# All softmax sums of an attention unit in one TensorE block: column groups by head and half, the fifth key block's values earlier

## The chip, the core and the metric

The kernel runs on one NeuronCore of a Trainium2 chip, in one launch. Times are device microseconds (us) of an execution. The engines are TensorE (PE in the profile; PEld is its weight load), VectorE (DVE), ScalarE (ACT), GpSimd (POOL) and SyncE (SP, which here only issues DMAs). Each works through its own queue in the order of the program; semaphores tie them together.

## What is computed

Sliding-window attention with a linear bias by distance, then a mixture-of-experts layer in which each token goes to one of 8 experts, all in float32:

```python
# q, k, v: (8, 8, 576, 64)
scores = scale * np.matmul(q, k.transpose(0, 1, 3, 2))
bias = slopes[:, None, None] * (-np.abs(rel).astype(np.float32))[None, :, :]
mask = (rel >= 0) & (rel < window)                       # window 128
scores = np.where(mask, scores + bias[None], -1000000000.0)
attn = np.exp(scores - np.max(scores, axis=-1, keepdims=True))
attn = attn / (np.sum(attn, axis=-1, keepdims=True) + 1e-09)
x = np.matmul(attn, v)                                   # -> (4608, 512)
...
h = np.maximum(x_sorted[lo:hi] @ w1[e], 0.0)             # the rows of expert e
y_sorted[lo:hi] = h @ w2[e]
...
return gate_w[:, None] * y
```

## The kernel before

**Units.** Attention is cut into 16 units. A unit `u` is two batch entries (`bp` is the pair, 0 to 3) and two heads (`hp` is the pair, 0 to 3), so four units in a row make one pair of batch entries. The 576 positions are nine key blocks of 64 (`kb`). A key block meets three query blocks of 64: its own and the next two. The queries are cut in two halves, `QH`: half 0 has 320 columns, half 1 has 256. Key blocks 0 to 4 reach into half 0, blocks 3 to 8 into half 1.

**Steps of a unit.**
- `scores` (matmuls at L790): q times k for one group of two key blocks (three in the last), as 64x64 matmuls, four of them side by side on the four quarters of the array. ACT takes the exponential (L799, L809), DVE multiplies by the bias factors (L803); the result is a probability tile `pe` of six buffers. Nothing is divided yet.
- `values` (L833): probabilities times v, again 64x64, into `at`, a PSUM tile with one buffer.
- `finish`: ACT copies `at` to SBUF (L850, L852). Then the sums of the probabilities over the keys (L864): matmuls of the probability tile with `ind`, 128 rows by 32 columns of weights, so that each writes 32 of the 128 output partitions, here called a column group (0 to 3). Head `r` and the parity of the key block choose the group: `j = 2 * r + kb % 2`. Half 0 begins with two matmuls of zeros (`none`), since odd key blocks don't reach its first 64 columns. ACT or DVE adds the result to `sumT` (L873, L875). The PSUM tile of the sums, `m`, has two buffers and is shared with the tasks below.

**Order.** The order is written out by hand (`manual_schedule`): each engine runs its instructions as the loop over `i = 4u + g` issues them. At step `g` of unit `u`:
- g = 0: one group of scores, values of key blocks 0, 1 (half 0)
- g = 1: values 2, 3 (half 0); a task; scores
- g = 2: values 4 (half 0); `finish(u, 0)`; a task; scores; values 3, 4, 5 (half 1)
- g = 3: values 6, 7, 8 (half 1); `finish(u, 1)`; a task; scores

Scores are issued ahead of their use: four groups, in units 0 and 1 three (L1417). SP's loads of the unit after the next are paced by probability tiles.

**Tasks.** When the four units of a pair of batch entries are done, `behind(bp)` (L1353) makes a list that `some()` (L1383) works off, one entry at each step: the gate's logits (`gate`, L884 matmuls in the same 128x32 shape as the sums, to groups 0 to 3 in turn; DVE adds L889, L891), their transposes on TensorE (`turn`, L908), routing on DVE, and the rows of x, transposed and written to DRAM. For `bp = 0` the rows are transposed on DVE (`squares_turned`, L1123) into tiles of the pool `rows`, which has four buffers; POOL copies the scales in (L1131) and issues the DMAs (L1142). The last of these nine tiles, tile 8, is left to the list of `bp = 1`, as `last` (L1374), which begins at unit 8. `scale_a` (L911) adds the two partial sums of a head, which lie in different column groups.

After the attention come the experts (two levels of seven-product matrix multiplication), with TensorE matmuls at L1527, L1590, L1629 and L1646. The change does not touch them.

Of the kernel before, what the change touches and what calls it, by code (L numbers as in the profile page):

```python
# [8 lines left out]
F32 = mybir.dt.float32  # L9
# [4 lines left out]
ALU = mybir.AluOpType  # L14
PSUM = bass.MemoryType.PSUM

P = 128
# [441 lines left out]
def kernel(  # L459
# [12 lines left out]
    nc = tc.nc  # L472
# [9 lines left out]
    KB = P // 2  # L482
    NK = S // KB
# [23 lines left out]
    with ExitStack() as fast:  # L507
# [70 lines left out]
        QH = [(0, 5 * KB), (5 * KB, 4 * KB)]  # L578

        ac = pool(att, "att_consts", 1)  # L580
# [9 lines left out]
        units = [(bp, hp) for bp in range(BP) for hp in range(HP)]  # L590
# [64 lines left out]
        for b in range(2):  # L655
            half = slice(b * KB, (b + 1) * KB)
# [14 lines left out]
        fac = ac.tile([P, H, GC], F32, name="fac")  # L671
# [17 lines left out]
        ind = ac.tile([P, HP, 32], F32, name="ind")  # L689
        nc.gpsimd.memset(ind[:], 0.0)  # L690
        for hp in range(HP):
            for b in range(2):
                nc.gpsimd.memset(ind[b * KB : (b + 1) * KB, hp, 16 + 2 * hp + b : 17 + 2 * hp + b], 1.0)
        none = ac.tile([P, 32], F32, name="none")
        nc.gpsimd.memset(none[:], 0.0)
        ident = consts.tile([P, P], F32, name="ident")
        make_identity(nc, ident[:])

# [80 lines left out]
        prob, xT, sumT, gs = {}, {}, {}, {}  # L779
# [34 lines left out]
        def by_distance(x, kb, a, b):  # L814

            if kb == NK - 1:
                return x[:, 5 * KB :].rearrange("p (j x) -> p j x", j=1)
            return x.rearrange("p (j k x) -> p j k x", j=3, k=2)[:, a:b, kb % 2, :]
# [22 lines left out]
        def finish(u, half):  # L841

            bp, hp = units[u]
            q0, qn = QH[half]
            if hp == 0 and half == 0:
                xT[bp] = xp.tile([P, HP, 2 * S], F32, name="xT")
                sumT[bp] = xp.tile([P, S], F32, name="sumT")
            acc = at.pop((u, half))[0]
            n = min(q0 + qn, LQ) - q0
            nc.scalar.copy(xT[bp][:, hp, : 2 * LQ].rearrange("p (b q) -> p b q", b=2)[:, :, q0 : q0 + n], acc[:, :, :n])  # L850
            if n < qn:
                nc.scalar.copy(xT[bp][:, hp, 2 * LQ :].rearrange("p (b q) -> p b q", b=2), acc[:, :, n:qn])  # L852
            sm = ps_m.tile([P, 512], F32, name="m")
            ops = []
            for kb in range(max(0, q0 // KB - 2), (q0 + qn) // KB):
                lo, hi = max(q0, kb * KB), min(q0 + qn, (kb + 3) * KB)
                ops.append((kb % 2, lo, hi, prob[4 * u + min(kb // 2, 3)], (kb, lo // KB - kb, hi // KB - kb)))
            if half == 0:
                ops.insert(0, (1, 0, KB, None, None))
            begun = set()  # L860
            for par, lo, hi, pe, at_kb in ops:
                for r in range(2):
                    j = 2 * r + par
                    nc.tensor.matmul(  # L864
                        sm[32 * j : 32 * j + 32, lo - q0 : hi - q0].rearrange("p (j x) -> p j x", x=KB),
                        lhsT=none[:] if pe is None else ind[:, hp, :],
                        rhs=fac[:, 0:1, :KB] if pe is None else by_distance(pe[:, r, :], *at_kb),
                        start=j not in begun, stop=True, skip_group_check=True,
                    )
                    begun.add(j)  # L870
            to = sumT[bp][:, q0 : q0 + qn]
            if hp == 0:
                nc.scalar.copy(to, sm[:, :qn])  # L873
            else:
                nc.vector.tensor_tensor(to, sm[:, :qn], to, op=ALU.add)  # L875


        def gate(bp, c):
            if bp not in gs:
# [31 lines left out]
        def scale_a(bp):  # L911
            G = gsr[bp]

            s = small.tile([P, TPB, 2, HP], F32, name="s")
            Gs = G.rearrange("p t (a k x) -> p t a k x", a=2, k=2)
            for t0, t1, p0, p1, b in ((0, 4, 0, P, 0), (4, 8, 0, P, 1), (8, 9, 0, KB, 0), (8, 9, KB, P, 1)):
                nc.vector.tensor_tensor(
                    s[p0:p1, t0:t1, :, :], Gs[p0:p1, t0:t1, :, 0, 16 + b : 24 + b : 2],
                    Gs[p0:p1, t0:t1, :, 1, 16 + b : 24 + b : 2], op=ALU.add,
                )  # L920
            low = small.tile([P, TPB * H], F32, name="low")
            sf = s.rearrange("p t a h -> p (t a h)")
            nc.vector.tensor_scalar(low[:], sf, scalar1=SUM_LO, scalar2=None, op0=ALU.is_ge)
            nc.vector.scalar_tensor_tensor(
                low[:], in0=sf, scalar=SUM_HI, in1=low[:], op0=ALU.is_le, op1=ALU.mult,
            )
            nc.vector.tensor_reduce(bad[:, bp : bp + 1], low[:], axis=AX, op=ALU.min)
            s_of[bp] = s
# [424 lines left out]
        def behind(bp):  # L1353

            g3 = [lambda k=k: gate(bp, k) for k in range(3)]
            t3 = [lambda k=k: turn(bp, k) for k in range(3)]
            rs = [lambda t=t: row(bp, t) for t in range(TPB)]
            a, a2, b, b2, c, n, q, p, p2, o, o2, e = (
                [lambda f=f: f(bp)] for f in (
                    scale_a, scale_a2, scale_b, scale_b2, scale_c, count, scales_squared, place, place2, ones_at,  # L1360
                    ones_at2, enlist,
                )
            )
            if bp == 0:
                rt = [lambda t=t: squares_turned(bp, t) for t in range(TPB)]
                ro = [
                    lambda t=t: (squares_scaled(bp, t), squares_out(bp, t, nc.gpsimd)) for t in range(TPB)
                ]
                return [g3[0:1], g3[1:2], g3[2:] + t3[0:1], t3[1:], a, a2, b, b2, c + n, rt[0:1], q + p + rt[1:2],
                        p2 + rt[2:4] + ro[0:2], o + ro[2:4], o2, rt[4:6] + ro[4:5], e + rt[6:8] + ro[5:8]]  # L1370
            rt, ro = ([lambda t=t, f=f: f(bp, t) for t in range(TPB)] for f in (row_turned, row_out))
            if bp == 1:
                last = [lambda: squares_turned(0, TPB - 1), lambda: squares_scaled(0, TPB - 1),
                        lambda: squares_out(0, TPB - 1, nc.gpsimd)]  # L1374
                return [g3[0:1], g3[1:2], g3[2:] + t3[0:1] + last, t3[1:], a + rt[0:1], a2 + rt[1:2], b + rt[2:3],
                        b2 + rt[3:4], c + n, [], p + ro[0:2], p2 + ro[2:4] + rs[4:5], o + rs[5:6], o2 + rs[6:7], rs[7:8],
                        e + rs[8:9]]
            return [g3, t3, a + a2, b + b2 + rt[0:1], c + n + rt[1:2], rt[2:4], p + p2 + ro[0:4], o + o2 + rs[4:6],
                    rs[6:9] + [early_holes], e + [early_table, lambda: gather(fixed[0], x_d[: 3 * 2 * S, :])]]
# [22 lines left out]
        for i in range(NG):  # L1402
            u, g = divmod(i, 4)
            bp, hp = units[u]
            if u + 2 < len(units):
                no_earlier_than(prob[i + 1][0:1, 0, 0:1])
                load_part(u + 2, g)
            if u in (10, 11) and g % 2 == 1:
                d = 2 * (u - 10) + g // 2
                load_w1(fixed[0], w1_a, slice(d, d + 1))  # L1410
            if i == 1:
                token_numbers()
                table_consts()
            if i == 12:
                token_parts()

            ahead = i + (3 if u < 2 else 4)  # L1417
            if g == 0:
                scores_to(ahead)
            if g == 0:  # L1420
                values(u, 0, (0, 1))
                if u < HP - 1:
                    factors(u + 1)
            elif g == 1:
                values(u, 0, (2, 3))
            elif g == 2:
                values(u, 0, (4,))
                finish(u, 0)
                some()
                scores_to(ahead)  # L1430
                values(u, 1, (3, 4, 5))
            else:
                values(u, 1, (6, 7, 8))
                finish(u, 1)
            if u in (13, 14):
                ws_tasks.pop(0)()
            if u == len(units) - 1 and g == 1:
                first = [t for _, t in prepare(fixed[0])]
                tasks.extend(first[:3])
            if g != 2:  # L1440
                some()
            if g in (1, 3):
                scores_to(ahead)
            if g == 3 and hp == HP - 1 and bp < BP - 1:
                tasks.extend(behind(bp))
# [270 lines left out]
        for i in range(len(groups)):  # L1716
# [3 lines left out]
            if i == 0:  # L1720
                strassen1(g, start=with_tail)
                todo = [t for _, t in prepare(fixed[1])]
                sums = [f for (f,) in todo[9:]]
# [64 lines left out]
```

## Time and profile before

| | us |
|---|---|
| median of 3 runs | 681.19 (678.4 to 684.45) |
| profiled execution | 676.36 |
| its span, first to last instruction | 674.6 |
| granted TensorE clock in it | 0.995 of full |

An instruction row of the profile's timeline reads: start, length, engine, line, operation, output and inputs, rows by columns of the weights for matmuls, shape, how many were merged, and in brackets the idle time of the engine before it with what ended that. A row of the groups reads: how many, busy time, mean duration in ns, idle time before them. A row of the waits reads: total, times, longest. Each float32 matmul shows as two rows of weight load and matmul. Ends of matmuls are modelled, and they overlap, so durations add up to more than the time that passes.

### The profile page before, as it was taken

The numbers are of one execution on the slowest core, as the hardware profiler recorded it, in microseconds if no ns is written. First come the engines' busy times: TensorE is split into PE (matmuls) and PEld (weight loads), VectorE is DVE, ScalarE is ACT, GpSimd is POOL, SyncE is SP. The second block draws the span as 40 slices with busy tenths as digits, with TensorE's granted clock in tenths as the row PEclk, the third lists the DMA queues.
The fourth block names the chain that finished last, engine by engine and source line by source line (L and its number), as shares of the span: only waits on it lengthen the run. The fifth ranks groups of instructions, "written<-read, shape, count | busy, mean of one in ns | idle before, by whom it ended". The sixth has DMA issues, their size and how long they took to land.

```text
span 674.6 us, 14825 instructions
## 1 busy us (share of the span) xinstructions
PE 648.4 (96%) x6004; PEld 541.2 (80%) x6004; DVE 362.1 (54%) x727; ACT 215.8 (32%) x493; POOL 272.7 (40%) x458
## 2 busy tenths in 40 slices
PE   6899999999999999999999999999999999999994
PEld 5768868687888888878878897889788788878892
DVE  3345956697797758436623841474356337614410
ACT  5757666675330331123012211311231023113100
POOL 8000682234032683575156426624760665230020
PEclk9999999999999999999999999999999999999998
DMA  9875998974358924673195439235822864282010
GB/s 267 226 190 170 256 246 256 374 217 133 125 121 304 332 62 145 215 284 110 63 313 178 149 93 320 98 141 191 302 63 99 281 218 148 60 298 112 1 64 8
DMA packets 55104, 122.02 MB, mean 181 GB/s; under 512 B 5905, under 2 KB 21425, under 8 KB 55026
## 3 DMA queue, kind: packets, MB, share of 16 engines
q1 hardware_dynamic: 43074, 92.51, 42.8%
q0 software_dynamic: 10800, 27.58, 12.8%
q8 instruction: 49, 0.80, 0.5%
q10 hardware_dynamic: 1152, 0.88, 0.4%
q14 instruction: 29, 0.24, 0.1%
HBM read 101.79 MB, written 19.96 MB: 180 GB/s over the span
## 4 chain that ended last, share of the span: by engine, by line
PE 74%; issue 10%; DVE 6%; DMA 3%; POOL 2%; ACT 1%; DVEq 0%; POOLq 0%; SPq 0%; ACTq 0%
PE pair1a L1590 5%; PE pair1b L1590 5%; PE pair0b L1527 4%; PE pair0a L1527 4%; PE pair2a L1527 4%; PE pair0a L1590 4%; PE pair0b L1590 4%; PE pair1b L1527 4%; PE pair2b L1527 4%; PE pair1a L1527 4%; PE pair2b L1590 4%; PE pair2a L1590 4%; PE sp L790 4%; PE at L833 3%; PE pair0a L1646 2%
## 5 line engine op out<-in xcount | busy, mean ns | idle before, releaser
L1278 POOL DMA_INDIRECT xg<-x_rows,p_idx x124 | 132.5, 1068 | 35.7 <-issue 33.3
L1613 POOL DMA_INDIRECT out_dram<-zo,s_idx x39 | 44.6, 1144 | 174.3 <-DVE zo L1604 136.8
L803 DVE TENSOR_TENSOR pe<-pe,fac 128x512 f32<-128x512 f32 x64 | 43.5, 686 | 46.0 <-ACT pe L799 45.1
L790 PE MATMUL sp<-q_sb,k_sb 64*64 64x192 f32 (+2 forms) x1152 | 54.9, 320 | 8.5 <-DMA q_sb<-in_qT_dram 5.7
L833 PE MATMUL at<-pe,v_sb 64*64 64x192 f32 (+2 forms) x1408 | 53.8, 282 | 2.4 <-issue 1.6
L833 PEld LDWEIGHTS at<-pe,v_sb 64*64 64x64 f32 x1408 | 45.6, 134 | 10.4 <-issue 3.6
L790 PEld LDWEIGHTS sp<-q_sb,k_sb 64*64 64x64 f32 x1152 | 39.9, 136 | 17.1 <-issue 5.8
L799 ACT ACTIVATE pe<-sp 128x512 f32<-128x512 f32 x64 | 38.5, 601 | 28.4 <-issue 12.1
L809 ACT ACTIVATE pe<-sp,mid 128x128 f32<-128x128 f32 x128 | 40.2, 374 | 0.0
L1538 ACT ACTIVATE h<-h 128x512 f32<-128x512 f32 x32 | 20.2, 630 | 38.6 <-DVE h L1537 38.6
L864 PE MATMUL m<-pe,ind 128*32 128x192 f32 (+2 forms) x704 | 29.4, 286 | 0.6 <-issue 0.6
L1142 POOL DMA_DIRECT2D x_rows<-xs x48 | 26.0, 553 | 7.3 <-DVE w L540 2.3
L1473 POOL COPY paced_by<-h 1x1 f32<-1x1 f32 x48 | 18.4, 383 | 23.0 <-DVE h L1637 16.5
L1296 DVE TENSOR_TENSOR xn<-xg 128x512 f32<-128x512 f32 x39 | 26.2, 674 | 2.5 <-DMA xg<-x_rows,p_idx 1.6
L864 PEld LDWEIGHTS m<-pe,ind 128*32 128x32 f32 x704 | 23.1, 109 | 2.9 <-issue 0.9
L1131 POOL COPY xs<-sq 128x16 f32<-128x16 f32 x10 | 3.2, 321 | 53.9 <-ACT sq L1109 53.9
L1312 DVE STREAM_TRANSPOSE xgT<-xn 128x512 f32<-128x512 f32 x31 | 22.1, 711 | 1.1
L538 DVE TENSOR_TENSOR w2s<-w 128x512 f32<-128x512 f32 x16 | 11.0, 685 | 20.5 <-DMA w<-in_moe_w_dram 20.5
L850 ACT COPY xT<-at 128x640 f32<-128x640 f32 (+1 forms) x32 | 19.0, 593 | 9.0 <-PE at L833 6.5
L1646 PE MATMUL pair2a<-w,h 128*128 128x512 f32 x48 | 21.1, 592 | 0.0
L1527 PE MATMUL pair0a<-xgT,w 128*128 128x256 f32 x72 | 17.1, 380 | 0.0
L1527 PE MATMUL pair0b<-xgT,w 128*128 128x256 f32 x72 | 17.1, 380 | 0.0
(381 smaller groups left out, 1407.7 us busy)
## 6 DMA issues: line engine op xcount, KB each, us to landing
w<-in_moe_w_dram SPq DMA_DIRECT2D x29, 2048.0 KB, 8.8
k_sb<-in_kT_dram SPq DMA_DIRECT2D x15, 576.0 KB, 7.8
q_sb<-in_qT_dram SPq DMA_DIRECT2D x15, 576.0 KB, 5.3
v_sb<-in_v_dram SPq DMA_DIRECT2D x14, 320.0 KB, 4.7
x_rows<-xs POOLq DMA_DIRECT2D x16, 264.0 KB, 5.2
v_sb<-in_v_dram SPq DMA_DIRECT2D x14, 256.0 KB, 4.6
x_rows<-xs POOLq DMA_DIRECT2D x32, 66.0 KB, 4.8
x_rows<-xT SPq DMA_DIRECT2D x8, 264.0 KB, 5.8
```

What stands on the lines that cost most here:

```text
L790: nc.tensor.matmul(by_distance(sp[c * KB : (c + 1) * KB, r, :GC], kb, 0, n), lhsT=k_sb[u][hs, c, kb * KB : (kb + 1) * KB], rhs=q_sb[u][hs, ...
L799: nc.scalar.activation(outer, sp[:, :, :GC].rearrange("p r (j x) -> p r j x", j=3)[:, :, 0:3:2, :], AF.Exp, scale=SCALE,)
L803: nc.vector.tensor_tensor(outer, outer, fac[:, h0 : h0 + 2, : 2 * w].rearrange("p r (j x) -> p r j x", j=2)[:, :, :, : 2 * KB], op=ALU.mult,)
L809: nc.scalar.activation(pe[:, r, inner], sp[:, r, inner], AF.Exp, bias=mid[:, h0 + r : h0 + r + 1], scale=SCALE,)
L833: nc.tensor.matmul(acc[r * D : (r + 1) * D, c, lo - q0 : hi - q0].rearrange("p (j x) -> p j x", x=KB), lhsT=v_sb[u // 2][c * KB : (c + 1) ...
L864: nc.tensor.matmul(sm[32 * j : 32 * j + 32, lo - q0 : hi - q0].rearrange("p (j x) -> p j x", x=KB), lhsT=none[:] if pe is None else ind[:, ...
L1278: nc.gpsimd.indirect_dma_start(out=to, out_offset=None, in_=where, in_offset=bass.IndirectOffsetOnAxis(ap=idx, axis=0),)
L1296: nc.vector.tensor_tensor(xn[:], x, s.unsqueeze(3).to_broadcast([P, NA, HP, TQ]), op=ALU.mult)
L1527: nc.tensor.matmul(ps[:, f * 256 : (f + 1) * 256], lhsT=left[m][:, d, fb * P : (fb + 1) * P], rhs=right[m][:, d, :], start=(m in (1, 2, 5) ...
L1590: nc.tensor.matmul(ps[:, :256], lhsT=left[m][:, f, c * P : (c + 1) * P], rhs=right[m][:, f, :], start=(m in (1, 2, 5) and f == 0), stop=Tr ...
L1613: ins = nc.gpsimd.indirect_dma_start(out=out[:, :], out_offset=bass.IndirectOffsetOnAxis(ap=s_idx[:, g["c0"] + j : g["c0"] + j + 1], axis= ...
L1646: nc.tensor.matmul(ps[:], lhsT=g["h"][:, fb, :], rhs=g["w2"][:, fb, :], start=(fb == 0), stop=(fb == FB - 1),)
```

## The change

The sums leave `finish` and become a function of their own, `sums(u)`, issued once a unit, at the beginning of g = 2: all key blocks, and in each the halves that it reaches. The column group is now chosen by half and head, `j = 2 * half + r`. Each group then receives all the key blocks of its head and half, the matmuls of zeros go away, and one PSUM tile holds the sums of the whole unit: half 0 in partitions 0 to 63, half 1 in 64 to 127. `sumT` keeps the same layout, and POOL sets the parts to zero that no sum reaches. Two evacuations of 64 partitions take the place of two of 128. `scale_a` adds the pairs of columns that now belong together.

The values of key block 4 move from g = 2 to g = 1, and `finish(u, 0)`, now only the copies, follows them there, ahead of that step's task and scores. In the list of `bp = 1`, `last` moves from the third entry to the first.

```diff
@@ finish / sums
             if hp == 0 and half == 0:
                 xT[bp] = xp.tile([P, HP, 2 * S], F32, name="xT")
                 sumT[bp] = xp.tile([P, S], F32, name="sumT")
+                for k in range(2):
+                    q0, qn = QH[1 - k]
+                    nc.gpsimd.memset(sumT[bp][k * KB : (k + 1) * KB, q0 : q0 + qn], 0.0)
...
+        def sums(u):
+
+            bp, hp = units[u]
             sm = ps_m.tile([P, 512], F32, name="m")
-            ops = []
-            for kb in range(max(0, q0 // KB - 2), (q0 + qn) // KB):
-                lo, hi = max(q0, kb * KB), min(q0 + qn, (kb + 3) * KB)
-                ops.append((kb % 2, lo, hi, prob[4 * u + min(kb // 2, 3)], (kb, lo // KB - kb, hi // KB - kb)))
-            if half == 0:
-                ops.insert(0, (1, 0, KB, None, None))
             begun = set()
-            for par, lo, hi, pe, at_kb in ops:
-                for r in range(2):
-                    j = 2 * r + par
-                    nc.tensor.matmul(
-                        sm[32 * j : 32 * j + 32, lo - q0 : hi - q0].rearrange("p (j x) -> p j x", x=KB),
-                        lhsT=none[:] if pe is None else ind[:, hp, :],
-                        rhs=fac[:, 0:1, :KB] if pe is None else by_distance(pe[:, r, :], *at_kb),
-                        start=j not in begun, stop=True, skip_group_check=True,
-                    )
-                    begun.add(j)
-            to = sumT[bp][:, q0 : q0 + qn]
-            if hp == 0:
-                nc.scalar.copy(to, sm[:, :qn])
-            else:
-                nc.vector.tensor_tensor(to, sm[:, :qn], to, op=ALU.add)
+            for kb in range(NK):
+                for half in range(2):
+                    q0, qn = QH[half]
+                    lo, hi = max(q0, kb * KB), min(q0 + qn, (kb + 3) * KB)
+                    if lo >= hi:
+                        continue
+                    pe = prob[4 * u + min(kb // 2, 3)]
+                    for r in range(2):
+                        j = 2 * half + r
+                        nc.tensor.matmul(
+                            sm[32 * j : 32 * j + 32, lo - q0 : hi - q0].rearrange("p (j x) -> p j x", x=KB),
+                            lhsT=ind[:, hp, :], rhs=by_distance(pe[:, r, :], kb, lo // KB - kb, hi // KB - kb),
+                            start=j not in begun, stop=True, skip_group_check=True,
+                        )
+                        begun.add(j)
+            for half in range(2):
+                q0, qn = QH[half]
+                rows_of = slice(half * KB, (half + 1) * KB)
+                to = sumT[bp][rows_of, q0 : q0 + qn]
+                if hp == 0:
+                    nc.scalar.copy(to, sm[rows_of, :qn])
+                else:
+                    nc.vector.tensor_tensor(to, sm[rows_of, :qn], to, op=ALU.add)
@@ scale_a
-                    s[p0:p1, t0:t1, :, :], Gs[p0:p1, t0:t1, :, 0, 16 + b : 24 + b : 2],
-                    Gs[p0:p1, t0:t1, :, 1, 16 + b : 24 + b : 2], op=ALU.add,
+                    s[p0:p1, t0:t1, :, :], Gs[p0:p1, t0:t1, 0, :, 16 + b : 24 + b : 2],
+                    Gs[p0:p1, t0:t1, 1, :, 16 + b : 24 + b : 2], op=ALU.add,
@@ behind
-                return [g3[0:1], g3[1:2], g3[2:] + t3[0:1] + last, t3[1:], a + rt[0:1], a2 + rt[1:2], b + rt[2:3],
+                return [last + g3[0:1], g3[1:2], g3[2:] + t3[0:1], t3[1:], a + rt[0:1], a2 + rt[1:2], b + rt[2:3],
@@ the loop
             elif g == 1:
-                values(u, 0, (2, 3))
+                values(u, 0, (2, 3, 4))
+                finish(u, 0)
             elif g == 2:
-                values(u, 0, (4,))
-                finish(u, 0)
+                sums(u)
                 some()
                 scores_to(ahead)
                 values(u, 1, (3, 4, 5))
```

More of the change, by code (lines that the diff above doesn't have):

```diff
@@ L693 @@
                 nc.gpsimd.memset(ind[b * KB : (b + 1) * KB, hp, 16 + 2 * hp + b : 17 + 2 * hp + b], 1.0)
-        none = ac.tile([P, 32], F32, name="none")
-        nc.gpsimd.memset(none[:], 0.0)
         ident = consts.tile([P, P], F32, name="ident")
```

## The prediction

> **What bounds the kernel now.** I read the page's engine shares and its chain of waits first, then the busy time by stretch, then TensorE's groups with shapes kept apart, then the timeline of single units.
>
> ```profile
> PE 648.4 (96%) x6004; PEld 541.2 (80%) x6004; DVE 362.1 (54%) x727; ACT 215.8 (32%) x493; POOL 272.7 (40%) x458
> PE 74%; issue 10%; DVE 6%; DMA 3%; POOL 2%; ACT 1%; DVEq 0%; POOLq 0%; SPq 0%; ACTq 0%
> 11.00:36.00 25.00, 18.99 (x512) 15.98 (x501) 8.84 (x14) 17.50 (x47) 5.64 (x54) 1.00 0.88 230
> 36.00:167.00 131.00, 125.67 (x2947) 101.77 (x2950) 89.24 (x225) 87.47 (x230) 44.94 (x91) 1.00 0.78 234
> 167.00:674.60 507.60, 497.69 (x2468) 418.58 (x2458) 259.76 (x470) 104.97 (x205) 212.96 (x270) 0.99 0.49 163
> ```
>
> The columns of the last three rows are the stretch, its length, and the busy time of PE, PEld, DVE, ACT and POOL. TensorE sets the end. The change lies in the attention, which ends near 167 us. From 36 us on PE is busy 125.67 of 131 us, so PE time added there reaches the end and PE time saved there mostly does. Before 36 us PE waits a quarter of the time while the DMA share is 0.88: units 0 to 2 are held by their loads, so I count 13 of the 16 units (3 to 15).
>
> ```profile
> L864 PE MATMUL m<-pe,ind 128*32 128x192 f32 x320 | 23.4, 328 | 0.0
> L864 PE MATMUL m<-pe,ind 128*32 128x128 f32 x192 | 19.3, 277 | 0.6 <-issue 0.6
> L864 PE MATMUL m<-pe,ind 128*32 128x64 f32 x192 | 13.9, 223 | 0.0
> 155.58 0.29 PE L833 MATMUL at<-pe,v_sb 64*64 64x64 f32 x8
> 155.81 0.25 PE L864 MATMUL m<-fac,none 128*32 128x64 f32 x2
> 155.82 0.36 PE L864 MATMUL m<-pe,ind 128*32 128x192 f32 x2
> 155.88 0.23 PE L864 MATMUL m<-fac,none 128*32 128x64 f32 x2
> 155.94 0.83 PE L864 MATMUL m<-pe,ind 128*32 128x192 f32 x18
> 156.70 0.88 PE L790 MATMUL sp<-q_sb,k_sb 64*64 64x192 f32 x16
> 157.58 1.55 PE L833 MATMUL at<-pe,v_sb 64*64 64x64 f32 x48
> 159.06 0.86 PE L864 MATMUL m<-pe,ind 128*32 128x64 f32 x24
> 159.85 1.54 PE L790 MATMUL sp<-q_sb,k_sb 64*64 64x192 f32 x40
> ```
>
> The groups show 704 passes for 352 matmuls of the program: each f32 matmul runs as two passes. A pass of 192, 128 or 64 columns takes 328, 277 or 223 ns: 0.82 ns a column and a fixed latency, which overlaps with the next pass. So a column group (32 output partitions) needs about 1.65 ns per column of a matmul. Below I use 0.833 ns a pass column.
>
> **One unit of before** (unit 14 above). Half 0's sums: from the start of the last value pass (155.58 + 0.29 - 0.22 = 155.65) to the first scores 1.05 us. Half 1's: from 158.91 (157.58 + 1.55 - 0.22) to 159.85, 0.94. Together 1.99 us. By columns the work itself is short, since consecutive blocks alternate between column groups {0, 2} and {1, 3}: half 0 has 448 columns on its fullest group (0.75 us), half 1 384 (0.64). The other 0.60 is two changes of array shape per block, 64x64 to 128x32 and back, 0.15 each.
>
> **The sums after the change.** Each of the four column groups gets 192 + 192 + 192 + 128 + 64 = 768 columns, 1.28 us if all four run side by side. But the order issued is groups 0, 1 for key blocks 0, 1, 2; all four for 3 and 4; groups 2, 3 for 5 to 8. How much overlaps depends on how far PE looks past work that waits for a busy group. Before never needs more than one block of lookahead, except in one place, where a gate follows the sums in the same shape:
>
> ```profile
> 51.63 0.77 PE L864 MATMUL m<-pe,ind 128*32 128x192 f32 x15
> 52.19 0.30 PE L884 MATMUL m<-xT,wgd 128*32 128x128 f32 x1
> 52.19 0.22 PE L864 MATMUL m<-pe,ind 128*32 128x64 f32 x1
> 52.20 0.30 PE L884 MATMUL m<-xT,wgd 128*32 128x128 f32 x1
> 52.23 0.23 PE L864 MATMUL m<-pe,ind 128*32 128x64 f32 x2
> 51.95 0.34 PEld L864 LDWEIGHTS m<-pe,ind 128*32 128x32 f32 x5
> 52.18 0.11 PEld L884 LDWEIGHTS m<-xT,wgd 128*32 128x32 f32 x1
> 52.20 0.21 PEld L884 LDWEIGHTS m<-xT,wgd 128*32 128x32 f32 x7
> ```
>
> The gate (L884) goes to groups 0, 1, 2, 3 in this order. Its matmuls on groups 1 and 3 start at 52.19 and 52.20, ahead of the last sums passes on groups 0 and 2 (52.23), which the program issues earlier. So groups do run out of program order. But not without limit: groups 1 and 3 had only their last 128-column pass left, and their next weights could have been loaded when it began, 0.11 us earlier. They were loaded at 52.18 and 52.20, as groups 0 and 2 began the first pass of their last block. At that moment group 0 had three passes queued behind the running one (one of the sums, two of the gate); just before it would have had four. I read from this that a group holds the running pass and three more, and that a fourth stops everything behind it in program order.
>
> With that rule the new order gives, by hand: the second pass of key block 3 on group 1 cannot be queued before that group's key block 2 begins at 0.64 us, so groups 2 and 3 start at 0.64 with 64 columns, then wait until 0.96 (key block 4 enters groups 0 and 1 only when their key block 3 begins), and then stream 128 + 192 + 192 + 128 + 64 = 704 columns, 1.17 us. The block lasts 2.13 us against 0.75 + 0.64 = 1.39: +0.74 a unit. Unlimited lookahead gives 1.28 (-0.11); none gives 2.35 (groups 0 and 1 through block 3, 704 columns, then groups 2 and 3 with 704): +0.96. I take +0.74, the value that fits the gate rows, and keep both ends.
>
> Against it, one block instead of two saves two shape changes, 0.30. Where a 128x128 transpose of a later stage follows half 1, one change remains; that is so in 9 of the 13 units, first and last:
>
> ```profile
> 55.85 0.86 PE L864 MATMUL m<-pe,ind 128*32 128x64 f32 x24
> 56.65 0.89 PE L908 MATMUL m<-ident,gs 128*128 128x128 f32 x5
> 166.45 0.86 PE L864 MATMUL m<-pe,ind 128*32 128x64 f32 x24
> 167.24 0.66 PE L1309 MATMUL m<-ident,xn 128*128 128x128 f32 x4
> ```
>
> So the sums cost 13 x (0.74 - 0.30) + 9 x 0.15 = +7.1 us. The removed `none` matmuls are in the 1.39 already: they ran on groups 1 and 3, beside 448 columns on 0 and 2.
>
> **The order around them.**
>
> ```profile
> PEld at L833 <- ACT xT L850: 3.0, 8, 0.5
> 157.58 1.41 PEld L833 LDWEIGHTS at<-pe,v_sb 64*64 64x64 f32 x48 [0.34 <-ACT xT L850]
> 156.82 0.70 ACT L850 COPY xT<-at 128x640 f32<-128x640 f32 x1
> 164.41 0.63 PE L1309 MATMUL m<-ident,xn 128*128 128x128 f32 x4 [0.81 <-DVE xn L1296]
> ```
>
> Half 1's values wait for ACT to empty the single `at` buffer, 8 times, 3.0 us in all; about 0.15 of each is the last scores streaming, so 8 x 0.2 = 1.7 us of PE. Here the copy stands behind the exponentials of the last scores (156.82 for values that ended at 155.87). After the change it is issued ahead of them, and scores and the whole sums block lie before its reader: -1.7. After half 1 the two copies lose the 0.94 us of sums that covered them, but two score groups remain (159.85 to 161.21, 1.36 us) against 0.20 + 0.75 of copies: 0, at most 0.3 a unit if ACT is late.
>
> Key block 4's values, and the sums' last key blocks, need probability tiles earlier than before. With scores four groups ahead, some 3 us of PE work lie between; for units 0 and 1, three ahead, there is a wait of up to 1 us each, in the stretch that the loads hold: 0.
>
> The wait for the gathered rows at 164.41 stands behind unit 15's half 0 sums; the longer block covers it: -0.8. Eight memsets on POOL (64 partitions, 320 or 256 columns) have their reader four units later: 0. The two evacuations of the sums have the same column counts and half the partitions: 0.
>
> **The moved task.** `last` (transpose of tile 8 on DVE, copy and 8 DMAs on POOL) goes from the third to the first place behind unit 7, ahead of the gate's DVE adds:
>
> ```profile
> 81.72 2.18 POOL L1142 DMA_DIRECT2D x_rows<-xs x4 [0.29 <-POOL xs L1131]
> 83.35 4.01 DMA x_rows<-xs
> 84.51 2.18 POOL L1142 DMA_DIRECT2D x_rows<-xs x4 [0.29 <-POOL xs L1131]
> 87.53 0.71 DVE L1123 STREAM_TRANSPOSE xs<-xT 128x512 f32<-128x512 f32 x1 [2.21 <-DMA x_rows<-xs]
> 89.34 1.28 DVE L889 TENSOR_TENSOR gs<-m,sumT 128x512 f32<-128x512 f32 x2
> 90.07 0.25 PE L864 MATMUL m<-fac,none 128*32 128x64 f32 x2 [0.86 <-DVE gs L889]
> ```
>
> Four buffers hold these tiles. Tile 7's transpose waited for tile 3's DMA (87.36). Tile 8's needs tile 4's: by the same delay from POOL's issue, 84.51 + 1.63 + 4.01 = 90.15. In DVE's queue it now stands before the gate's add (89.34), and unit 8's sums wait for that add's PSUM buffer (90.07): they would start 90.15 + 0.71 + 0.7 = 91.5, 1.45 later. POOL's chain started at unit 6, and PE comes 2 x 0.4 us later by the sums themselves: net +0.6. POOL's own order is the same.
>
> **Sum.** 7.1 - 1.7 - 0.8 + 0.6 = +5.2 us. The profiled execution took 676.4 us (span 674.6, 1.8 around it): 681.6. It stands 4.8 below the median of the runs (681.19), so on that scale I predict 686.4 us, 0.8% above.
>
> **Rivals.**
> *All four groups overlap.* The gate's late weight loads have another cause, and a group can run any number of passes ahead. Then the sums take 1.28 us: 13 x (-0.11 - 0.30) + 1.35 - 1.7 + 1.8 (the DVE wait at unit 8 in full, and a little more, since POOL's chain does not get faster) = -3.9, so 677.3. For it: L884 does overtake L864. Against: the loads at 52.18. [...]
>
> *No overlap, slower.* If a matmul starts only when all before it have started, groups 2 and 3 run after groups 0 and 1: 2.35 us, 13 x 0.22 = 2.9 more, 689.3: slower by 1.2%. It decides from a block of about 2.25 us on. For it: everything in before except the gate fits it too. Against: 52.19 before 52.23. [...]
>
> *The change is absorbed.* If the attention's end is held by the chain of DMA and POOL that shows in the waits of unit 8 and of the gather, PE's extra time fills waits and the time stays: about 682. Against: PE waits under 6 of 131 us.
>
> **How the numbers follow.** Forecast 0.55, all four overlap 0.17, none (or less than I read) 0.2, absorbed 0.08. A measurement of this kernel can tell about 1% (6.8 us) from no change; the three runs spread by 6. Around the forecast I put 2.5 us, so it lies above 688 in about a quarter of its cases. Slower by over 1%: 0.14 + 0.13 = 0.27. Faster by over 1% (under 674.4): an eighth of the full overlap, and a little for the unknown, 0.05. The rest, 0.68, within 1%. The range 676.5 to 691 takes in both ends of the lookahead; the likeliest case alone has 683 to 690.
>
> **What would show it.** In the changed profile: L864 in one run of 44 passes a unit, from first to last start 2.0 to 2.1 us (1.25 if all overlap, 2.3 if none), groups 2 and 3 starting about 0.64 in. No wait of L833 on L850. A wait of unit 8's sums on the gate's add of 1 us or more, behind a transpose on DVE. The stretch after 167 us (507 us long) unchanged. The prediction is wrong if the block is near 1.3 us, or if new waits for ACT appear ahead of half 0's values.

## The result and the profile after

The changed kernel took 689.36 us (median of 9 runs, 686.27 to 691.36) against 681.93 for the kernel before on the same chip (9 runs, 678.4 to 684.45): ratio 1.010, 95% interval 1.0075 to 1.0124. All ratios here are of undisturbed executions; one of the twelve of the kernel called "all three undone" below took 3798.45 us and does not enter its ratio. The forecast was 686.4, 0.8% slower. The profiled execution took 687.5 us, its span is 685.8 us, and 11.2 us more than the span before. These are the rows of the page and of the busy time by stretch, cut at 11 and 36 us as before and at the end of the attention (the columns are stretch, length, busy PE, PEld, DVE, ACT, POOL, then the granted clock):

```profile
PE 660.7 (96%) x5940; PEld 547.5 (80%) x5940; DVE 364.3 (53%) x727; ACT 216.7 (32%) x493; POOL 278.3 (41%) x465
11.00:36.00 25.00, 22.26 (x551) 18.59 (x547) 8.74 (x14) 16.73 (x45) 7.17 (x59) 1.00 0.81 225
36.00:179.68 143.68, 134.73 (x2873) 105.61 (x2869) 91.97 (x227) 88.87 (x231) 48.12 (x95) 0.99 0.75 215
179.68:685.80 506.12, 497.70 (x2470) 418.70 (x2462) 259.32 (x469) 105.19 (x205) 213.89 (x270) 1.00 0.49 163
```

The experts' part is the same within 1.5 us (506.12 against 507.60). The whole loss lies in the attention: 12.7 us. At 36 us the two kernels do not stand at the same point of the program (551 passes of PE against 512 since 11 us), so the first two stretches are best taken together: from 11 us to the end of the attention PE is busy 156.99 us against 144.66 before, 12.3 more, and idle 11.7 against 11.3. That busy time is not the sums alone: a stretch at half clock and the bursts near the end, both described below, are in it. The next rows are from PE's timeline of the changed kernel, units 3 and 4, the second with a gate behind the sums:

```profile
41.19 2.40 PE L869 MATMUL m<-pe,ind 128*32 128x192 f32 x44
43.52 0.88 PE L788 MATMUL sp<-q_sb,k_sb 64*64 64x192 f32 x16
...
51.34 2.18 PE L869 MATMUL m<-pe,ind 128*32 128x192 f32 x38
53.26 0.30 PE L890 MATMUL m<-xT,wgd 128*32 128x128 f32 x2
53.35 0.28 PE L869 MATMUL m<-pe,ind 128*32 128x128 f32 x2
53.39 0.28 PE L890 MATMUL m<-xT,wgd 128*32 128x128 f32 x2
53.46 0.28 PE L869 MATMUL m<-pe,ind 128*32 128x64 f32 x4
```

All 44 passes of a unit's sums run in one stretch of 2.40 us, 2.18 from first to last start (the last pass of 64 columns takes 0.22). The forecast for this was 2.0 to 2.1. By the starts of the single passes in the trace, the first passes of groups 2 and 3 (64 columns, unit 3) begin 0.69 us in, where 0.64 was forecast. The gate's matmuls (L890) again start ahead of sums that are issued before them (L869 at 53.35).

PE's waits in the changed kernel show what the forecast did not have:

```profile
PE at L831 <- DVE pe L801: 4.0, 4, 2.4
PE m L869 <- ACT xs L1080: 0.5, 1, 0.5
PE at L831 <- ACT xT L853: 0.2, 1, 0.2
```

The wait of half 1's values for the copy of `at` is gone. (The 0.2 left is half 0's values of unit 15, which wait for half 1's second copy.) In its place the values of half 0, now with key block 4 at g = 1, wait for their probability tile, 4.0 us in all, four times (0.5 us, twice, before). The longest is at unit 8; these are its rows on DVE and on PE:

```profile
89.42 0.71 DVE L1129 STREAM_TRANSPOSE xs<-xT 128x512 f32<-128x512 f32 x1 [1.79 <-DMA x_rows<-xs]
90.05 1.25 DVE L801 TENSOR_TENSOR pe<-pe,fac 128x512 f32<-128x512 f32 x2
91.84 0.71 DVE L1129 STREAM_TRANSPOSE xs<-xT 128x512 f32<-128x512 f32 x1 [0.54 <-DMA x_rows<-xs]
92.48 1.39 DVE L895 TENSOR_TENSOR gs<-m,sumT 128x512 f32<-128x512 f32 x2
```

```profile
90.76 0.49 PE L831 MATMUL at<-pe,v_sb 64*64 64x64 f32 x8 [2.35 <-DVE pe L801]
91.17 1.93 PE L890 MATMUL m<-xT,wgd 128*32 128x512 f32 x8
93.04 1.23 PE L788 MATMUL sp<-q_sb,k_sb 64*64 64x192 f32 x16
94.20 2.18 PE L869 MATMUL m<-pe,ind 128*32 128x192 f32 x38
```

Tile 7's transpose (89.42) waits 1.79 us for the DMA that frees its buffer. The multiply that finishes the probability tile (90.05) stands behind it in DVE's queue, and PE stands behind that, 2.35 us. Tile 8, the moved task, comes second (91.84), ahead of the gate's add.

### The profile page after: what moved, and what is told of

Same layout as the page of the kernel before. It is cut to its first block, busy times and chain, and to the rows that moved or that the text cites. A ratio compares the mean times of both kernels' runs of the same rounds, so it can differ in the third digit from the quotient of the medians.

```text
span 685.8 us, 14723 instructions
## 1 busy us (share of the span) xinstructions
PE 660.7 (96%) x5940; PEld 547.5 (80%) x5940; DVE 364.3 (53%) x727; ACT 216.7 (32%) x493; POOL 278.3 (41%) x465
## 4 chain that ended last, share of the span: by engine, by line
PE 76%; issue 9%; DMA 4%; DVE 4%; POOL 2%; ACT 1%; another core or an unknown queue 1%; ACTq 0%; SPq 0%; DVEq 0%; POOLq 0%
PE pair1a L1596 5%; PE pair1b L1596 5%; PE pair0b L1533 4%; PE pair0a L1533 4%; PE sp L788 4%; PE m L869 4%; PE pair2a L1533 4%; PE pair0a L1596 4%; PE pair0b L1596 4%; PE pair1b L1533 4%; PE pair2b L1533 4%; PE pair1a L1533 4%; PE pair2b L1596 4%; PE pair2a L1596 4%; PE at L831 3%
## 5 line engine op out<-in xcount | busy, mean ns | idle before, releaser
L788 PE MATMUL sp<-q_sb,k_sb 64*64 64x192 f32 (+2 forms) x1152 | 56.7, 322 | 7.8 <-DMA q_sb<-in_qT_dram 5.0
L869 PE MATMUL m<-pe,ind 128*32 128x64 f32 (+2 forms) x704 | 38.6, 286 | 0.5 <-ACT xs L1080 0.5
L869 PEld LDWEIGHTS m<-pe,ind 128*32 128x32 f32 x704 | 29.1, 109 | 11.3 <-issue 3.0
L1479 POOL COPY paced_by<-h 1x1 f32<-1x1 f32 x48 | 20.2, 421 | 23.0 <-DVE h L1643 16.5
L1087 POOL COPY xs<-es 128x16 f32<-128x16 f32 x18 | 7.3, 405 | 32.4 <-issue 14.5
```

The lines of the kernel that those rows point to most:

```text
L788: nc.tensor.matmul(by_distance(sp[c * KB : (c + 1) * KB, r, :GC], kb, 0, n), lhsT=k_sb[u][hs, c, kb * KB : (kb + 1) * KB], rhs=q_sb[u][hs, ...
L869: nc.tensor.matmul(sm[32 * j : 32 * j + 32, lo - q0 : hi - q0].rearrange("p (j x) -> p j x", x=KB), lhsT=ind[:, hp, :], rhs=by_distance(pe ...
```

## The experiments

Every ratio below is to the kernel before on the same chip, in the same job. The kernel before had medians of 682.19, 677.47 and 681.9 us in the three jobs, so times of different jobs are compared by ratio only.

### How far ahead a column group runs: four orders of the sums

The first edit lets the two sides alternate:

```diff
-            for kb in range(NK):
-                for half in range(2):
+            for kb, half in ((0, 0), (3, 1), (1, 0), (4, 1), (2, 0), (5, 1), (3, 0), (6, 1), (4, 0), (7, 1), (8, 1)):
```

> The changed kernel with the sums' key blocks issued in another order, halves in turn (0/half 0, 3/half 1, 1/half 0, 4/half 1, ...), so that column groups {0,1} and {2,3} alternate. Theory A (a column group holds the running pass and three more, a fourth stops everything behind it): the block falls from 2.24 to about 1.35 us in each unit, 13 x 0.9 = 11 us less than the changed kernel, about 678 to 680. Rival B (matmuls start in program order): 1.60 plus start, about 1.7 us a block, about 682. Rival C (the block's length does not matter, DVE and DMA hold the units): block shorter, time stays near 689.

Measured: 682.87 us, ratio 1.0005 (0.9982 to 1.0028). The block came out as expected, the time did not: by the ratios it is 6.5 us under the changed kernel, not 11. From PE's timeline, unit 5 of this kernel:

```profile
62.97 1.54 PE L867 MATMUL m<-pe,ind 128*32 128x192 f32 x44
64.43 0.88 PE L788 MATMUL sp<-q_sb,k_sb 64*64 64x192 f32 x16
```

The block takes 1.54 - 0.22 = 1.32 us from first to last start. The same 44 passes on the same groups, in another order, are 0.86 us shorter. The other two orders:

```diff
# halves: half 0 whole, then half 1 whole
+            for kb, half in ((0, 0), (1, 0), (2, 0), (3, 0), (4, 0), (3, 1), (4, 1), (5, 1), (6, 1), (7, 1), (8, 1)):
# pairs: two key blocks a side in turn
+            for kb, half in ((0, 0), (1, 0), (3, 1), (4, 1), (2, 0), (3, 0), (5, 1), (6, 1), (4, 0), (7, 1), (8, 1)):
```

> Only the order of the sums is changed: half 0 whole (key blocks 0 to 4 on groups 0 and 1), then half 1 whole (3 to 8 on groups 2 and 3). Theory A (a group holds the running pass and three more, a fourth blocks all that follows): groups 2 and 3 start 0.96 us after the first pass plus start-up, about 1.0, and the block lasts 2.24 by columns, 2.29 from first to last start when the 0.10 by which the block of the changed kernel exceeded its rule is added in the same way. Rival B (two waiting passes): 2.40. Rival C (four): 2.13, groups 2 and 3 starting at 0.8. Rival D (strict program order): groups 2 and 3 start when the last pass of groups 0 and 1 starts, 1.1, block 2.5. Rival E (groups wholly independent): 1.3 as in the alternating order. Time of the kernel: one to two us over the changed kernel's.

> Only the order of the sums is changed: two key blocks for groups 0 and 1, two for groups 2 and 3, and so on. By columns the fullest group still has 1.28 us. Theory A (three waiting passes): 1.60 by columns, 1.65 from first to last start, since the second pair of each side comes in late; groups 2 and 3 start at once, then have a gap from about 0.27 to 0.64. Rival B (two waiting): 1.81. Rival C (four waiting): 1.49, the gap ending at 0.48. Rival D (program order): 1.97. Rival E (independent): 1.3.

Measured: one run each, 683.18 and 676.61 us (before in that job 677.47). PE's timeline of the order by halves, then of the order by pairs:

```profile
60.56 2.52 PE L867 MATMUL m<-pe,ind 128*32 128x192 f32 x44
63.01 0.88 PE L788 MATMUL sp<-q_sb,k_sb 64*64 64x192 f32 x16
```

```profile
58.88 1.86 PE L867 MATMUL m<-pe,ind 128*32 128x192 f32 x44
60.67 0.88 PE L788 MATMUL sp<-q_sb,k_sb 64*64 64x192 f32 x16
```

Both blocks came out as expected for three waiting passes (2.29 and 1.65). The table sets the four orders beside five rules, all from first to last start in us. The rules count columns alone, less the last pass, at the prediction's estimate of 0.833 ns a pass column (in unit 3 of the changed kernel a group's second pass starts 0.187 us after its first, and the further ones of 192 columns start 0.162 to 0.163 us after one another, 0.85 ns a column); "program order" takes the two passes of a matmul together:

| order | program order | two waiting | three waiting | four waiting | no limit | measured |
|---|---|---|---|---|---|---|
| as changed | 2.30 | 2.19 | 2.08 | 1.92 | 1.23 | 2.18 |
| halves | 2.40 | 2.30 | 2.19 | 2.03 | 1.23 | 2.30 |
| pairs | 1.87 | 1.71 | 1.55 | 1.39 | 1.23 | 1.64 |
| alternating | 1.55 | 1.39 | 1.23 | 1.23 | 1.23 | 1.32 |

Three passes waiting behind the running one fits all four with the same excess, 0.09 to 0.11 us a block. Two waiting is met in two rows, but the other two are shorter than it allows. The starts of single passes in the changed kernel's trace show the depth directly (unit 3). Eight passes stand ahead of the first ones of groups 2 and 3 on group 1, and these begin (at 0.686 us) 5 ns after the fifth of the eight; ten stand ahead of their first passes of key block 4, and these begin (at 1.011) 5 ns after the seventh. Each time three are left waiting. So the depth is three in these blocks, and what was sized too low is a tenth of a microsecond, nearly the same in all four. In strict program order alternating would take at least 1.55; it took 1.32.

### Undoing one move at a time

```diff
# values of key block 4 and the copies back to g = 2, ahead of the sums
-                values(u, 0, (2, 3, 4))
-                finish(u, 0)
+                values(u, 0, (2, 3))
             elif g == 2:
+                values(u, 0, (4,))
+                finish(u, 0)
                 sums(u)
```

> The changed kernel with the values of key block 4 and the copy of half 0 back at step 2, just ahead of the sums. Theory A: the new waits of the values on DVE's probability tiles (4.0 us, 2.4 of it in unit 8) had come from the earlier place; they go, and 2 to 4 us with them: about 686. Rival: the sums at step 2 then wait for the same tiles, or the values of half 1 wait for ACT again (8 x 0.2): no gain, 688 to 690.

```diff
# tile 8 behind the gate's first step
-                return [last + g3[0:1], g3[1:2], g3[2:] + t3[0:1], t3[1:], a +
+                return [g3[0:1] + last, g3[1:2], g3[2:] + t3[0:1], t3[1:], a +
```

> The changed kernel with the moved task (tile 8's transpose, scales and DMAs) behind the gate's first matmuls and DVE add in the same step, instead of ahead of them. Theory A: unit 8's gate add no longer waits for tile 4's DMA and the transpose, about 1 us less: 688.3. Rival: unit 8 is held by the values' wait for DVE (behind tile 7's transpose), which does not move: 0.

Measured: values back 687.6 us, ratio 1.0087 (1.0064 to 1.0111); tile 8 later 687.1, ratio 1.0068 (1.0046 to 1.009). Neither undoes the loss. Unit 8 shows why. PE's timeline with the values back, then with tile 8 later:

```profile
89.42 0.34 PE L831 MATMUL at<-pe,v_sb 64*64 64x64 f32 x8 [0.86 <-DVE pe L801]
91.66 3.71 PE L869 MATMUL m<-pe,ind 128*32 128x192 f32 x38 [1.90 <-DVE gs L895]
```

```profile
91.63 0.34 PE L831 MATMUL at<-pe,v_sb 64*64 64x64 f32 x8 [2.97 <-DVE pe L801]
93.72 2.18 PE L869 MATMUL m<-pe,ind 128*32 128x192 f32 x38
```

With the values back, they wait 0.86, but the sums wait 1.90 for the gate's add behind tile 8's transpose. With tile 8 later, the sums do not wait, but the values wait 2.97 behind tile 7's. Together 2.8 and 3.0 us, against 2.35 in the changed kernel's first profile and 2.09 + 1.05 in its second: the same rows of x, written by the same chain of POOL and DMA, hold PE at either place.

### All three undone, and the sums alone

The alternating order, the values back at g = 2, and `last` back in third place:

> Sums alternating as in the first, the values of key block 4 and the copy back at step 2 as in the second, and the moved task back in its third place. Theory A: gains add, 689.4 - 11 - 3 - 0.5, about 675: one block a unit in place of two, all groups side by side, faster than the kernel before (682) by about 1%. Rival: the cover of the copy of half 0 shrinks with the block (1.3 us and one group of scores) and ACT's copy is waited for again, 2 us given back: 677.

Measured: 679.89 us, ratio 0.9953 (0.9927 to 0.9979): half a percent faster than the kernel before, but not the 675 or 677 us that were expected.

The changed order of the sums kept, only the two moves taken back:

```diff
-                return [last + g3[0:1], g3[1:2], g3[2:] + t3[0:1], t3[1:], a +
+                return [g3[0:1], g3[1:2], g3[2:] + t3[0:1] + last, t3[1:], a +
# and values of key block 4 with finish(u, 0) at g = 2, as above
```

> The changed order of the sums stays; the fifth block's values and the last tile of rows go back to where they were. Theory: these two moves cost the same wait once (values of half 0 behind a transpose on DVE), so the time goes to 686.5 to 687.5, as with either alone. Rival: they cost separately and the gains add, 1.8 and 2.3: 685.0 to 685.5. Second rival: the sums' order alone makes the loss, and neither counts: 689.

Measured: 678.4 us, ratio 1.0019 (0.9999 to 1.004). All three outcomes that this expectation names (686.5 to 687.5, 685.0 to 685.5, 689) were wrong, also on the scale of this job, where the changed kernel would stand near 684: taking both moves back is worth far more than either undone alone had shown. So the question turned round, and the last job put the parts beside the whole.

### The parts beside the whole

The kernel before with only the moves. Its two blocks of sums become a function and keep their old places:

```diff
             elif g == 1:
-                values(u, 0, (2, 3))
+                values(u, 0, (2, 3, 4))
+                finish(u, 0)
             elif g == 2:
-                values(u, 0, (4,))
-                finish(u, 0)
+                sums(u, 0)
...
-                return [g3[0:1], g3[1:2], g3[2:] + t3[0:1] + last, t3[1:], a +
+                return [last + g3[0:1], g3[1:2], g3[2:] + t3[0:1], t3[1:], a +
```

> The kernel before with only the moves: values of the fifth block and the copies of half 0 at g = 1, the last tile of rows first in its list; the sums stay two blocks a unit in their old groups. Theory M (the moves make most of the loss: values that wait for a probability tile behind a transpose on DVE, at unit 8 above all, while the longer sums mostly fill waits that were there): slower than the kernel before by 3 to 6 us, ratio 1.004 to 1.009, with a wait of 2 us or more ahead of half 0's values in unit 8. Theory S (the sum on record: moves +0.6, wait for the copy -1.7): ratio 0.998 to 1.000.

> The changed kernel once more, beside the parts on the same chip: ratio to before 1.007 to 1.012. With theory M it is near the sum of the gains over before of the moves alone and of the sums alone; with theory S it is near the sums alone. Its profile also shows whether the bursts of scores near 169 us belong to it: if so, 3 to 4 us between unit 14 and unit 15 as before; if they belong to the chip, they are here and in the kernel before alike, or in neither.

> The changed sums with both moves taken back, once more, beside the changed kernel and the moves alone. Theory M: ratio to before 1.000 to 1.004, 4 us or more under the changed kernel. Theory S: within 1 us of the changed kernel.

Measured, before at 681.9 us (24 runs):

| kernel | us | ratio | 95% interval |
|---|---|---|---|
| moves alone | 684.59 | 1.0037 | 1.0007 to 1.0066 |
| sums alone | 683.6 | 1.0020 | 0.9994 to 1.0047 |
| changed kernel | 687.61 | 1.0089 | 1.0056 to 1.0122 |

The ratio of the moves alone excludes a gain from them (the theory of the sum on record); at 2.5 us the loss is a little under what theory M expected, and so is the wait at unit 8 (1.50). The sums alone cost 1.4 us by the ratio, a result that cannot be told from zero, and the same as in the job before (1.0019). The two parts add to 0.0057 and the whole is 0.0089; whether they add or make each other worse, the intervals leave open.

Where the time goes is seen between two equal points of the program, the first values of unit 4 and of unit 14. The rows, in this order: the kernel before in this job, the sums alone, the moves alone, the changed kernel.

```profile
44.65:149.52 104.87, 99.68 (x2288) 79.20 (x2283) 72.78 (x188) 70.37 (x186) 36.84 (x79) 1.00 0.82 248
```

```profile
46.21:152.68 106.47, 104.38 (x2253) 83.25 (x2249) 73.40 (x186) 70.97 (x186) 37.55 (x82) 1.00 0.81 245
```

```profile
46.62:152.78 106.16, 99.49 (x2287) 78.70 (x2283) 72.74 (x188) 71.05 (x186) 36.78 (x79) 1.00 0.81 245
```

```profile
46.63:156.50 109.87, 104.69 (x2247) 82.43 (x2243) 73.48 (x186) 71.12 (x186) 39.23 (x82) 1.00 0.79 237
```

The same for all profiles, in us; idle is length less PE's busy time. Each kernel has one or two profiles, and the three of the kernel before differ by 2.3 us in length and 1.0 in busy time, so only differences within one job are read closely:

| ten units | length | PE busy | PE idle |
|---|---|---|---|
| before (three profiles) | 103.5, 105.8, 104.9 | 99.4, 100.4, 99.7 | 4.1, 5.4, 5.2 |
| sums alone (two) | 106.5, 107.6 | 104.4, 104.4 | 2.1, 3.2 |
| moves alone | 106.2 | 99.5 | 6.7 |
| changed (two) | 111.4, 109.9 | 105.8, 104.7 | 5.5, 5.2 |
| values back | 110.9 | 105.8 | 5.2 |
| tile 8 later | 111.3 | 104.7 | 6.5 |
| order by halves | 112.0 | 105.9 | 6.1 |
| order by pairs | 107.7 | 101.3 | 6.4 |
| alternating order | 105.3 | 96.6 | 8.7 |
| all three undone | 103.3 | 97.2 | 6.1 |

The first profile of the changed kernel, values back and order by pairs have a stretch at half clock in these units (mean granted clock 0.98), which makes PE about 1 us busier (105.8 against 104.7 in the changed kernel). The sums alone make PE 4.0 and 4.7 us busier than before in the same job, and 2.2 and 3.1 of that vanish in waits that were there already: the length grows by 1.8 and 1.6. The moves alone add no work and 1.5 us of waiting. In the changed kernel the same work of the sums is there, and the waits are back at 5.2: all of it shows. With one move undone the length is 111; with both, in the later jobs, it is 106.5 and 107.6. The main ones of PE's waits over those ten units, in the same order of kernels:

```profile
PE m L908 <- DVE gs L891: 0.9, 2, 0.5
PE m L864 <- DVE gs L889: 0.8, 1, 0.8
PE m L995 <- DVE sumT L875: 0.6, 1, 0.6
PE m L1072 <- ACT xs L1074: 0.6, 1, 0.6
PE m L864 <- ACT xs L1074: 0.5, 1, 0.5
PE at L833 <- ACT xT L850: 0.4, 1, 0.4
```

```profile
PE m L869 <- DVE gs L895: 0.9, 1, 0.9
PE m L914 <- DVE gs L897: 0.8, 2, 0.4
PE m L1001 <- DVE sumT L882: 0.2, 1, 0.2
```

```profile
PE at L833 <- DVE pe L803: 3.3, 4, 1.5
PE m L869 <- DVE gs L894: 1.4, 1, 1.4
```

```profile
PE at L831 <- DVE pe L801: 2.8, 3, 2.1
PE m L869 <- DVE gs L895: 1.0, 1, 1.0
```

With the sums alone the waits for ACT's scaled rows, for `sumT` and for the copy are gone or down to 0.2, while those for the gate's adds stay: it seems that a longer block on PE gives ACT and DVE the time. Both kernels with the moves have the wait for the probability tile instead, and in these two profiles no wait of 0.2 us or more for the scaled rows (the changed kernel's first profile has one of 0.5). So each part alone fills these old waits, and together they can fill them only once; that would make the whole more than the sum of its parts. No run tests it, and the intervals leave the sizes open.

### Two more profiles of the kernel before

> The kernel before, unchanged, for a second profiled execution. Theory: the bursts of five score passes with gaps of about half a us under 'issue', seen near 169 us in the changed kernel and at two places in the alternating one, are not of the change; then this profile shows such bursts too, somewhere, and its span is nearer 680 than 674.6. Rival: they come with the change's longer program; then the span is within 1 us of 674.6 and the scores after unit 14 stream as in the first profile.

> The kernel before on this chip, for its profile: if the changed kernel shows the bursts of scores near 169 us in this job and this one doesn't, they belong to the change; if both or neither do, they don't. Waits of TensorE in units 7, 11 and 15 of 0.5 to 1.3 us each, on ACT and on the gathered rows, which the longer sums would fill.

Measured: 677.47 us, span 675.7, without bursts; and 679.39 us, span 677.6, with bursts. From PE's timelines, the second profile of the two and then the changed kernel's first:

```profile
162.43 0.55 PE L833 MATMUL at<-pe,v_sb 64*64 64x192 f32 x4 [0.19 <-issue]
163.18 0.56 PE L833 MATMUL at<-pe,v_sb 64*64 64x192 f32 x5 [0.20 <-issue]
```

```profile
171.72 0.56 PE L788 MATMUL sp<-q_sb,k_sb 64*64 64x192 f32 x5 [0.18 <-issue]
172.47 0.54 PE L788 MATMUL sp<-q_sb,k_sb 64*64 64x192 f32 x5 [0.19 <-issue]
```

Four to six passes every 0.75 us, under "issue". They are in all four profiles of the last job, with the change and without it, and in none of the four of the job before, three of which have changed sums. Three profiles of the first job show them too (values back, tile 8 later, all three undone). So they do not belong to the change. The first profile of the kernel before lacks them and the changed kernel's first has them; that puts some 4 us of the 11.2 between these two spans (the changed kernel is 6.5 us behind at unit 14 and 10.1 at unit 15, by the first values of half 1, counted from unit 3 and against the profile of 675.7). Of the waits looked for here, those of units 11 and 15 were there (0.6 for ACT, 0.65 for the gathered rows); that of unit 7 was not.

## Why the prediction was right, point by point

**The total.** +5.2 us was forecast; +7.4 was measured beside the first result and +6.1 in the last job (0.0089 of 681.9). The range held, and the new order's extra PE work, which was to make the loss, is there. But two terms were off in opposite directions, and that the total came out near is in part luck: alone, the sums cost 1.4 us where +4.6 stood on record, and the moves 2.5 us where +0.6 less the copy's 1.7 stood.

**What a column group holds.** Right for these sums, and now shown by four orders: the running pass and three more. The block came out 0.10 us longer than by columns, as did every other order's. Each of the two old blocks has 0.06 of such an excess too (0.75 and 0.64 from first to last start, against 0.69 and 0.59 by columns), so the difference a unit was close: PE's busy time grew by 0.40 to 0.47 us a unit with the sums alone, against 0.44 to 0.59 forecast.

**"PE time added there reaches the end."** This is the step that failed for the sums. On record they made, with the copy's and the gather's gain, 7.1 - 1.7 - 0.8 = +4.6. Alone they cost +1.3 and +1.4 (0.0019 and 0.0020 of their job's before; the intervals end at 2.7 and 3.2). The work is there (4.0 to 4.7 us in ten units); 2.2 to 3.1 us of it fell into waits. Beside the copy's, these were the waits for the scaled rows and for `sumT`, which the prediction did not look at one by one. Its rival "absorbed" was right for this part in its outcome, though not in the waits that it named (those of unit 8 and of the gather).

**The wait for the copy of `at`.** Right that it goes: the weight loads of the values waited 3.0 us for it before, and 0.3 for half 1's second copy after. That it was worth 1.7 us of PE no run shows by itself.

**Key block 4's values one step earlier, costed at nothing.** This is the other step that failed. "Some 3 us of PE work lie between" counted only PE's work, not what stands in DVE's queue ahead of the multiply: transposes that wait for a DMA (unit 8, where PE waits 2.35 us in the first profile), the routing's small operations (unit 6, 0.58), and at unit 11 a late exponential (0.82). It costs 4.0 us of waiting in the first profile of the changed kernel and 3.1 in the second, against 0.5 before.

**The moved task, +0.6.** Its mechanism is there: tile 8's transpose stands ahead of the gate's add, and the sums wait 1.90 with the values back and 1.39 with the moves alone, against 0.8 to 0.9 before. In the changed kernel most of it hides behind the values' wait at the same unit, since both wait for the same chain: the sign that was named, a wait of unit 8's sums of 1 us or more, is absent in its first profile and is 1.05 in its second. The two moves together cost 2.5 us alone (0.5 to 4.5) and were put at 0.6 less the copy's 1.7. `last` alone in its old place was not tried: with the copies at g = 1 the rows that it still has to read would be overwritten.

**The stretch behind the attention.** Unchanged, as forecast.

**The rivals.** "All four overlap" and "no overlap" both fell: 2.18 us is neither 1.25 nor 2.3, and alternating gives 1.32. But the first one's sign is what the alternating order can bring: with the moves undone it gives 0.9953. Even there PE's busy time falls by 7.2 us in the ten units against the sums alone, and the length by 3.2 to 4.3 (profiles of different jobs).

## What to carry to other kernels

Where the order of matmuls on several column groups is free, look whether one group's passes hold back another's: in these sums a fourth pass behind the running one did, and alternating the groups took the block from 2.18 to 1.32 us without changing any work. A consumer that moves earlier must be followed through the queue of its producer's engine, past every instruction there that can itself wait for a DMA: PE's distance in work says nothing of that (some 3 us of it was counted on here, and PE waited 2.35 us at unit 8). And where PE is 96% busy, as here, ask of each remaining wait whether another chain (a DMA, ACT, POOL) or PE's own progress sets its end: in the two comparisons here added work disappeared into the first kind and saved work turned into it, and some 0.35 to 0.6 of a change in busy time reached the length.

## What the runs showed of the hardware

The depth of the lookahead, in this kernel's 128x32 sums: three waiting passes a column group, with a fourth holding back all that follows on other groups. The blocks of the four orders (2.18, 2.30, 1.64 and 1.32 us) follow it to 0.01 us once the 0.10 is taken off. Between column groups PE does not start matmuls in the order of the program (L890 at 53.26 us, ahead of L869 at 53.35, which is issued before it).

The granted clock. In the changed kernel's first profile it rises at 11.89 us, falls to 0.50 at 90.40, rises again at 93.81 and falls at 680.90: 23, 1 and 172 times 3.413 us. In the first profile of the kernel before it rises at 9.26 and falls at 668.04, 193 times that. Below, such a stretch of 3.41 us, counted from these changes, is called a slot. These are the changed kernel's slots around the 2.35 us wait at unit 8, and then, for tile 8 later, two stretches of the same length across which its wait of 2.97 us lies:

```profile
86.98:90.40 3.42, 1.42 (x24) 0.51 (x16) 1.63 (x3) 0.65 (x3) 3.12 (x7) 1.00 0.89 242
90.40:93.81 3.41, 3.05 (x28) 1.13 (x32) 2.82 (x5) 0.69 (x1) 3.12 (x7) 0.50 0.74 173
```

```profile
86.70:90.11 3.41, 1.97 (x32) 0.67 (x24) 0.71 (x1) 1.19 (x4) 2.59 (x6) 1.00 0.75 185
90.11:93.52 3.41, 1.89 (x32) 0.88 (x32) 2.49 (x4) 0.00 (x0) 2.89 (x7) 1.00 0.81 218
```

In the first, a slot with 1.42 us of PE work is followed by a slot at half clock, in which the scores stream at half speed: passes of 192 columns start 0.320 us apart (93.41 to 93.73), against 0.163 at full clock (43.74 to 43.90). In the other the longer wait is split between two stretches with 1.97 and 1.89 us of work, and the clock stays; so it does after a wait of 2.09 us at the same unit in the changed kernel's second profile and after one of 2.47 in the order by halves, while one of 2.16 in the order by pairs is followed by a fall to 0.50. In the first profiles of the two kernels the slots at full clock with 0.85, 1.03 and 1.42 us of PE work were each followed by one at 0.50, and none of the others was, the least busy of them with 1.76 and 1.77. So the length of a wait alone did not decide it; that its place in the slots counts as well is an estimate from these few.

The bursts of four to six passes every 0.75 us near the end of the attention come and go with the job, for the kernel before too, and cost some 3 to 4 us. What makes them was not found.
